# Moving attention steps of two batches to other slots of the channel MLP that hides them

## The chip, the cores and the metric

One core of a Trainium2 chip runs the whole kernel. The metric is the device time of one execution in microseconds (us). TensorE (PE) does the matrix products, VectorE (DVE), ScalarE (ACT) and GpSimd (POOL) the element-wise work, and SyncE (SP) issues nearly all DMAs.

## The reference

For 8 batches of 8 heads, 576 tokens and 64 features a head, a linear attention with cosine weights feeds an MLP-mixer block:

```python
phi(x)  = concat(relu(x) * cos_w, relu(x) * sin_w)        # 64 -> 128 features
kv, z   = sum_s phi(k) v^T,  sum_s phi(k)
attn    = (phi(q) kv) / (phi(q) z + 1e-6)                 # x: [B, 576, 512] after joining the heads
u       = x + (relu(x^T @ w_tok1) @ w_tok2)^T             # token MLP, 576 -> 256 -> 576
out     = u + relu(u @ w_ch1) @ w_ch2                     # channel MLP, 512 -> 1536 -> 512
```

## The kernel before

The 576 tokens of a batch are laid out as J = 4 full tiles of 128 rows and a half tile, so attention runs over JA = 5 tiles. The half tiles of two neighbouring batches share one tile (`u_tail`), whose channel MLP comes at the very end. All products take bf16 operands.

The channel MLP is most of the work of TensorE, and everything else is fitted between its matmuls. `channel` walks through 24 or 20 slots:

- Slots 0 to 11: one of 12 chunks of the hidden layer each. Four 128x512 matmuls fill `c_ps`, and a relu evacuates it to `h1`, on ACT for a letter "A" and on DVE for a "D" in a string given by the caller. For batch 0 that is `AAAAAAAADDAD`, for batch 1 `AAAAAADADADA`.
- The slots after: the second product into `o_ps`. In batch 0 (`wide`) all four output tiles advance together, one hidden chunk a slot (slots 12 to 23). In the other batches the tiles come one by one, six matmuls a slot, two slots a tile (12 to 19). DVE adds `u` and SP stores.

After each slot, `step()` calls the hooks registered for it. The hooks are the attention and token-MLP steps of the batches to come. In this document "channel p" is the channel MLP of batch p; in its hooks `n` is batch p+1, whose attention and token MLP have to be complete when channel p ends, and `m` (called `n2` in channel 0) is batch p+2, which is prepared. The schedule is manual, so each engine runs its instructions in the order in which they are written, and a waiting instruction holds up all that is written after it for its engine.

The steps of a batch, as methods of `Batch`:

- `k_feature(j)`: two DVE instructions that build the cosine and sine halves of `kp` for tile j. `q_feature(j)`: the same for `qp`, both halves on ACT, or one of them on DVE with `dve=(1,)`.
- `v_cast(j, eng)`: casts one tile of v to bf16, on POOL unless another engine is named.
- `q_turn(j, n)`: transposes `qp` into `qpT`. Batches 2 to 7 do it by DMA from SP; batch 1 does it on TensorE into a PSUM tile of pool `psA`, which ACT then copies (L256).
- `kv_mm`: 40 small matmuls into `kv_ps` (pool `psA`) and one evacuation by ACT (L270). It needs all five tiles of `kp` and of the cast v.
- `num(j)`: 8 matmuls into `nm` (pool `psA`), then three DVE instructions that divide and write `x`.
- `mix1(j)`, `mix1_out`: the first product of the token MLP, accumulated over the tiles, and its relu `B1`.
- `mix2(g)`: the second product into `u_ps`; DVE adds x, POOL casts to `ub`, and `ub` is transposed into `uT`, the operand of the next channel's first product. Batches 2 to 7 transpose it by DMA (L371), batch 1 on TensorE with a copy by ACT (`u_turn`, L375 and L376).

The pool `psA` has two buffers of two banks, `psM` four of one bank. `qp`, `kp` and `ub` have one buffer each, `qpT`, `x`, `u` and `uT` two. The raw v is one tile for all batches; raw k and q have two.

Of the kernel before, what the change touches and what calls it, by code (L numbers as in the profile page):

```python
# [9 lines left out]
F32 = mybir.dt.float32  # L10
# [5 lines left out]
def kernel(  # L16
# [11 lines left out]
    nc = tc.nc  # L28

    B, H, S, D = q.shape  # L30
    Dm = H * D
    _, D_tok = moe_w_tok1.shape
    _, D_ch = moe_w_ch1.shape
    P = 128
    J = S // P
    JA = J + 1
# [4 lines left out]
    NCH = D_ch // P  # L41
# [3 lines left out]
    U_PE = (1,)  # L45
# [4 lines left out]
    def first(c):  # L50

        return (0, JA - c)

    def count(c, par):
        return JA if par == c else J
# [6 lines left out]
    psM = ctx.enter_context(tc.tile_pool(name="psM", bufs=4, space=bass.MemoryType.PSUM))  # L62
# [87 lines left out]
    for par_ in range(2):  # L150
        n, f = count(0, par_), first(0)[par_]
        d = nc.gpsimd.dma_start(out=w1[0][par_::2, :n],
                                in_=moe_w_tok1.rearrange("(m r) t -> m r t", r=R)[:, f:f + n, :])
# [6 lines left out]
    for g in range(3):  # L160
        cs = slice(g * D_ch // 3, (g + 1) * D_ch // 3)
        wc1_dma.append(nc.gpsimd.dma_start(out=wc1[:, :, cs],
                                           in_=moe_w_ch1[:, cs].rearrange("(n p) c -> p n c", p=P)))
    wc2 = const.tile([P, NCH, Dm], BF16, name="wc2")
# [5 lines left out]
    for c in range(2):  # L170
        for par_ in range(2):
            n, f = count(c, par_), first(c)[par_]
# [203 lines left out]
            nc.scalar.copy(dst, tr)  # L376


    def channel(uT, u, store, by_slot, hooks, wide=False):
        h1 = one.tile([P, NCH, 4 * P], BF16, name="h1")  # L380
        slot = 0

        def step():
            nonlocal slot
            for f in hooks.get(slot, ()):
                f()
            slot += 1

        for mi in range(NCH):
            c_ps = psM.tile([P, 4, P], F32, name="c_ps", tag="psM")  # L390
            for ki in range(NCC):
                nc.tensor.matmul(c_ps, wc1[:, ki, mi * P:(mi + 1) * P], uT[:, :, ki, :],  # L392
                                 start=(ki == 0), stop=(ki == NCC - 1))
            src = c_ps.rearrange("p a b -> p (a b)")
            if by_slot[mi] == "A":
                nc.scalar.activation(h1[:, mi, :], src, AF.Relu)  # L396
            else:
                nc.vector.tensor_relu(h1[:, mi, :], src)
            step()
        if wide:  # L400
            o_ps = [psM.tile([P, Dm], F32, name="o_ps", tag="psM") for j in range(4)]
            for ki in range(NCH):
                for j in range(4):
                    nc.tensor.matmul(o_ps[j], h1[:, ki, j * P:(j + 1) * P], wc2[:, ki, :],  # L404
                                     start=(ki == 0), stop=(ki == NCH - 1))
                step()
            for j in range(4):
                nc.vector.tensor_add(u[:, j, :], o_ps[j], u[:, j, :])
                store(j, u)
            return  # L410
        for j in range(4):
            o_ps = psM.tile([P, Dm], F32, name="o_ps", tag="psM")
            for half in range(2):
                for ki in range(half * NCH // 2, (half + 1) * NCH // 2):
                    nc.tensor.matmul(o_ps, h1[:, ki, j * P:(j + 1) * P], wc2[:, ki, :],  # L415
                                     start=(ki == 0), stop=(ki == NCH - 1))
                if half:
                    nc.vector.tensor_add(u[:, j, :], o_ps, u[:, j, :])  # L418
                    store(j, u)
                step()  # L420

    def out_rows(b, par, j, n):
        f = first(b % 2)[par] + j
        return out[b].rearrange("(m r) c -> m r c", r=R)[:, f:f + n, :]

    def store_batch(b):
        def store(j, u):
            if j % 2:
                for par in range(2):
                    nc.sync.dma_start(out=out_rows(b, par, j - 1, 2), in_=u[par::2, j - 1:j + 1, :])  # L430
        return store

    def store_tail(j, u):
        for c, eng in ((0, nc.sync), (1, nc.scalar)):
            eng.dma_start(out=out_rows(2 * j + c, c, J, 1), in_=u[c::2, j:j + 1, :])


    bt = [Batch(b) for b in range(B)]
# [33 lines left out]
    def first_hooks(n, n2):  # L472
        h = {}

        def at(slot, f, *a, **kw):
            h.setdefault(slot, []).append(lambda: f(*a, **kw))
        for g in range(3):
            at(1 + g, bt[0].mix2, g, turn=False)
        for j in range(JA):
            at(3 + j, n.k_feature, j)  # L480
            at(7 + j, n.q_feature, j, dve=(1,))
            at(9, n.v_cast, j)
        at(10, n.q_turn, 0, 2)
        at(11, n.q_turn, 2, 2)
        at(11, load, 2, "v")
        at(12, n.q_turn, 4, 1)
        at(12, n.kv_mm)
        for j in range(JA):
            at(13 + j, n.num, j)
            at(15 + j, n.mix1, j)  # L490
        at(19, n.mix1_out, split=True)
        for g in range(3):
            at(20 + g, n.mix2, g)
        at(20, n2.q_feature, 0)
        at(21, n2.q_feature, 1)
        at(21, load, 3, "k")
        at(21, load, 3, "q")
        return h

    def second_hooks(n, m):  # L500
        h = {}

        def at(slot, f, *a, **kw):
            h.setdefault(slot, []).append(lambda: f(*a, **kw))
        for j in range(JA):
            at(j, n.k_feature, j)
            at(j, n.v_cast, j)
        for j in range(2, JA):
            at(j - 2, n.q_feature, j)
        at(0, n.q_turn, 0, 2)  # L510
        at(1, n.q_turn, 2, 2)
        at(2, n.q_turn, 4, 1)
        at(5, n.kv_mm)
        at(5, load, 3, "v")
        at(5, load, 4, "k")
        at(5, load, 4, "q")
        for j in range(JA):
            at(6 + j, n.num, j)
            at(8 + j, n.mix1, j)
            at(6 + j, m.q_feature, j)  # L520
            at(7 + j, m.v_cast, j)
            at(13 + j, m.k_feature, j)
        at(12, m.q_turn, 0, 2)
        at(12, n.mix1_out)
        at(13, m.q_turn, 2, 2)
        at(13, load, 4, "v")
        for g in range(3):
            at(13 + g, n.mix2, g)
        at(16, m.q_turn, 4, 1)
        return h  # L530

    def hooks_for(n, m, nxt):

        h = {}

        def at(slot, f, *a, **kw):
            h.setdefault(slot, []).append(lambda: f(*a, **kw))
        if nxt is not None:
            at(0, load, nxt, "k")
            at(0, load, nxt, "q")  # L540
            at(9, load, nxt, "v")
        if n is not None:
            at(0, n.kv_mm)
            for j in range(JA):
                at(2 + j, n.num, j)
            for j in range(JA):
                at(7 + j // 3, n.mix1, j)
            at(8, n.mix1_out)
            at(10, n.mix2, 0)
            at(11, n.mix2, 1)  # L550
            at(12, n.mix2, 2)
        if m is not None:
            for j in range(JA):
                at(3 + j, m.v_cast, j)
                at(9 + j, m.q_feature, j)
                at(13 + j, m.k_feature, j)
            at(12, m.q_turn, 0, 2)
            at(15, m.q_turn, 2, 2)
            at(16, m.q_turn, 4, 1)
        return h  # L560

    evac = ["A"] * 7 + ["D", "A", "D", "D", "D"]
    for p in range(B):
        s = bt[p]
        if p == 0:
            channel(s.uT, s.u, store_batch(p), list("AAAAAAAADDAD"), first_hooks(bt[1], bt[2]), wide=True)
            if 1 in U_PE:
                bt[1].u_turn(0)
                bt[1].u_turn(1)
        elif p == 1:  # L570
            channel(s.uT, s.u, store_batch(p), list("AAAAAADADADA"), second_hooks(bt[2], bt[3]))
        else:
            n = bt[p + 1] if p + 1 < B else None
            m = bt[p + 2] if p + 2 < B else None
            nxt = p + 3 if p + 3 < B else None
            channel(s.uT, s.u, store_batch(p), evac if n else ["A", "D"] * 6, hooks_for(n, m, nxt))
    channel(uT_tail, u_tail, store_tail, ["A", "D"] * 6, {})

    _ = tile, bass_utils
# [30 lines left out]
```

## Time and profile before

| | |
|---|---|
| median of 3 runs | 285.31 us (284.68 to 285.60) |
| span of the profiled execution | 282.6 us |
| busy: PE, DVE, ACT, POOL | 264.9, 167.2, 118.8, 56.4 us |
| channel 0, from its first matmul to that of channel 1 | 25.79 to 63.51 us |
| channel 1 | 63.51 to 98.41 us |
| channel 2 | 98.41 to 126.17 us |
| channel 3 | 126.17 to 153.75 us |

Times in the trace are us from the start of the span. A line of the timeline gives the start, the length, the engine, the line of the kernel, the operation and how many instructions were merged; in brackets stands how long the engine had been idle, and which engine's instruction released it. A line of waits gives who waited for whom, the total, the number of waits and the longest. A line of windows gives, for a stretch, its length, the busy time of each engine with its number of instructions, the clock granted to TensorE as a share of full speed, and the DMA load.

### The profile page before, as it was taken

To read this page: it belongs to the slowest core of one execution; us is meant where nothing else is said; L and a number is where in the kernel's file an instruction comes from. 1 tells how busy PE (TensorE), PEld (TensorE's weight loads), DVE (VectorE), ACT (ScalarE), POOL (GpSimd) and SP (SyncE) were. 2 spreads that over 40 slices of the span, in tenths; PEclk is the share of its full clock that TensorE was granted. 3 is DMA by queue.
4 is the path that set the end of the run, shared out by engine and by line. 5 is a ranking of instruction groups with operands and counts; after the bars stand their busy time and mean duration, and the time that the engine had idled before them with its cause. 6 is when DMAs were issued, how large, how long until landed. Compare 5 with 4: busy or idle time off the path is not lost.

```text
span 282.6 us, 4609 instructions
## 1 busy us (share of the span) xinstructions
PE 264.9 (94%) x1801; PEld 131.6 (47%) x1822; DVE 167.2 (59%) x331; ACT 118.8 (42%) x175; POOL 56.4 (20%) x83
## 2 busy tenths in 40 slices
PE   8979998979789899999999999999999999999993
PEld 2554455445333364446445544554455444444441
DVE  4774883587638645985587659665747553423321
ACT  2873493258590055805570556156515201301300
POOL 4472360052042400530061006100200120000000
PEclk9999999999997999999999999999999999999999
DMA  6999997998999999399969994940691063003012
GB/s 212 321 156 269 362 220 212 359 303 227 196 367 224 299 281 340 76 194 247 364 145 213 294 317 96 206 128 2 110 249 53 0 95 149 1 26 125 0 74 75
DMA packets 78567, 53.62 MB, mean 190 GB/s; under 512 B 47761, under 2 KB 75729, under 8 KB 78545
## 3 DMA queue, kind: packets, MB, share of 16 engines
q1 hardware_dynamic: 74608, 49.06, 62.8%
q0 software_dynamic: 3616, 3.74, 8.4%
q10 hardware_dynamic: 320, 0.52, 0.5%
q8 instruction: 14, 0.23, 0.3%
q14 instruction: 9, 0.07, 0.1%
HBM read 35.78 MB, written 9.44 MB: 160 GB/s over the span
## 4 chain that ended last, share of the span: by engine, by line
PE 65%; DMA 2%; ACT 1%; DVE 1%; POOL 0%; SPq 0%; issue 0%; DVEq 0%
PE o_ps L415 26%; PE c_ps L392 26%; PE u_ps L343 4%; PE nm L280 2%; PE kv_ps L265 2%; DMA uT<-ub 2%; PE ut_ps L355 1%; PE b_2301 L300 1%; PE b_1986 L300 1%; PE b_2606 L300 1%; PE b_1671 L300 1%; PE b_1352 L300 1%; DVE u L345 0%; POOL ub L348 0%; SPq L371 0%
## 5 line engine op out<-in xcount | busy, mean ns | idle before, releaser
L392 PE MATMUL c_ps<-uT,wc_135 128*128 128x512 bf16 x384 | 93.4, 379 | 2.9 <-ACT uT L376 1.6
L392 PEld LDWEIGHTS <-wc_135 128*128 128x128 bf16 x432 | 39.7, 98 | 45.8 <-DMA uT<-ub 1.8
L348 POOL CAST ub<-u 128x1024 bf16<-128x1024 f32 x14 | 14.7, 1049 | 129.0 <-DVE u L345 74.0
L418 DVE TENSOR_TENSOR u<-o_ps,u 128x512 f32<-128x512 f32 x28 | 19.3, 689 | 23.9 <-PE o_ps L415 23.8
L288 DVE TENSOR_TENSOR x<-nm,den 128x512 bf16<-128x512 f32 x40 | 27.7, 692 | 1.4
L345 DVE TENSOR_TENSOR u<-u_ps,x 128x1024 f32<-128x1024 f32 x16 | 19.5, 1222 | 6.0 <-PE u_ps L343 6.0
L284 DVE TENSOR_SCALAR den<-nm 128x8 f32<-128x8 f32 x40 | 6.6, 166 | 27.0 <-PE nm L280 27.0
L280 PEld LDWEIGHTS <-qpT 128*128 128x128 bf16 x320 | 14.8, 98 | 13.5 <-issue 2.8
L280 PE MATMUL nm<-kv,qpT 128*128 128x65 bf16 x320 | 16.8, 194 | 2.9 <-ACT kv L270 1.4
L236 ACT ACTIVATE qp<-qt_79,bias_108,cos_t 128x512 bf16<-128x512 f32 x20 | 15.9, 804 | 3.5 <-DMA qpT<-qp 3.5
L223 POOL CAST vbf_125<-vt_77 128x512 bf16<-128x512 f32 x20 | 13.6, 723 | 16.7 <-DMA vt_77<-in_v_dram 15.3
L236 ACT ACTIVATE qp<-qt_76,bias_108,cos_t 128x512 bf16<-128x512 f32 x19 | 15.0, 803 | 0.5 <-DMA qt_76<-in_q_dram 0.5
L415 PE MATMUL o_ps<-wc_139,h_844 128*128 128x512 bf16 x47 | 12.2, 401 | 1.4 <-ACT h_844 L396 1.3
L396 ACT ACTIVATE h_1186<-c_ps 128x512 bf16<-128x512 f32 x8 | 4.8, 597 | 19.6 <-issue 14.3
L265 PEld LDWEIGHTS <-kp 128*128 128x128 bf16 x320 | 11.1, 97 | 3.3 <-ACT qpT L256 1.2
L138 PE MATMUL wm<-zero 128*128 128x512 bf16 x37 | 11.0, 467 | 1.4 <-POOL zero L70 1.3
L396 ACT ACTIVATE h_2730<-c_ps 128x512 bf16<-128x512 f32 x6 | 3.6, 597 | 20.6 <-PE c_ps L392 20.6
L236 ACT ACTIVATE qp<-qt_76,bias_108,sin_t 128x512 bf16<-128x512 f32 x15 | 12.0, 803 | 0.0
L236 ACT ACTIVATE qp<-qt_79,bias_108,sin_t 128x512 bf16<-128x512 f32 x15 | 12.0, 801 | 0.0
L404 PE MATMUL o_ps<-wc_139,h_441 128*128 128x512 bf16 x45 | 11.8, 379 | 0.2
L215 DVE TENSOR_SCALAR kp<-kt_75,cos_t 128x512 bf16<-128x512 f32 x18 | 10.3, 571 | 2.5 <-DMA kt_75<-in_k_dram 2.5
L215 DVE TENSOR_SCALAR kp<-kt_78,sin_t 128x512 bf16<-128x512 f32 x20 | 11.0, 551 | 0.0
(146 smaller groups left out, 394.0 us busy)
## 6 DMA issues: line engine op xcount, KB each, us to landing
out_dram<-u SPq DMA_DIRECT2D x32, 256.0 KB, 2.6
vt_77<-in_v_dram SPq DMA_DIRECT2D x8, 640.0 KB, 9.2
vt_77<-in_v_dram SPq DMA_DIRECT2D x8, 512.0 KB, 9.0
kt_75<-in_k_dram SPq DMA_DIRECT2D x4, 640.0 KB, 6.8
qt_76<-in_q_dram SPq DMA_DIRECT2D x4, 640.0 KB, 9.4
kt_78<-in_k_dram SPq DMA_DIRECT2D x4, 640.0 KB, 7.2
qt_79<-in_q_dram SPq DMA_DIRECT2D x4, 640.0 KB, 9.3
kt_75<-in_k_dram SPq DMA_DIRECT2D x4, 512.0 KB, 5.2
```

What stands on the lines that cost most here:

```text
L215: eng.tensor_scalar(dst, src, scalar1=tab, scalar2=0.0, op0=ALU.mult, op1=ALU.max)
L223: eng.tensor_copy(self.vb[:, j, :, :D], src)
L236: nc.scalar.activation(self.qp[:, j, :, f, :], src, AF.Relu, bias=bias0, scale=tab[:, self.c, j:j + 1])
L265: nc.tensor.matmul(kv_ps[:, g, hh * (D + 1):(hh + 1) * (D + 1)], self.kp[:, j, h].rearrange("p f d -> p (f d)"), self.vb[:, j, h, :D + 1], ...
L280: nc.tensor.matmul(nm[:, h // HH, c0:c0 + D + 1], lw, self.kv[:, h, :D + 1], start=True, stop=True)
L288: nc.vector.tensor_mul(self.x[:, j, :].rearrange("p (g h d) -> p g h d", g=2, h=HH), nmv[:, :, :, :D], den_b)
L300: nc.tensor.matmul(self.b1[mi], w1[self.c][:, j, mi * P:(mi + 1) * P], self.x[:, j, :], start=(j == 0), stop=(j == J))
L345: nc.vector.tensor_add(self.u[:, js, :], u_ps, self.x[:, js, :])
L348: nc.gpsimd.tensor_copy(self.ub[:, js, :], self.u[:, js, :])
L392: nc.tensor.matmul(c_ps, wc1[:, ki, mi * P:(mi + 1) * P], uT[:, :, ki, :], start=(ki == 0), stop=(ki == NCC - 1))
L415: nc.tensor.matmul(o_ps, h1[:, ki, j * P:(j + 1) * P], wc2[:, ki, :], start=(ki == 0), stop=(ki == NCH - 1))
L418: nc.vector.tensor_add(u[:, j, :], o_ps, u[:, j, :])
```

## The change

The change moves hooks of channel 0 and channel 1 to other slots. No operation is added or taken away in the work that runs. Its aim is to put work that isn't urgent (features and turns of a later batch) behind what TensorE waits for, and to spread the casts of v.

In channel 0: q features of batch 1 one slot earlier; its v casts in slot 10 in place of 9, with tiles 0 to 2 on POOL, tile 3 on DVE and tile 4 on ACT; `kv_mm` ahead of the second and third q turn, in slot 11 in place of 12; `num`, `mix1`, `mix1_out` and `mix2` one slot earlier; the two `u_turn` of batch 1 inside the last two slots, where they had come after the whole channel.

In channel 1: the q features of batch 3 in slots 13 to 17, behind the last relu evacuation of slot 11, where they had stood in slots 6 to 10 between the evacuations; its q turns in slots 15, 17 and 18 (12, 13 and 16 before); its k features one slot later.

It also gives `channel` an argument `fine` and `store_tail` an argument `cs`. No call sets `fine`, and `cs` keeps its default, so neither changes an instruction. They are left out below.

```diff
@@ first_hooks (channel 0; n is batch 1, n2 is batch 2)
         for j in range(JA):
             at(3 + j, n.k_feature, j)
-            at(7 + j, n.q_feature, j, dve=(1,))
-            at(9, n.v_cast, j)
-        at(10, n.q_turn, 0, 2)
+            at(6 + j, n.q_feature, j, dve=(1,))
+            at(10, n.v_cast, j, (nc.gpsimd, nc.gpsimd, nc.gpsimd, nc.vector, nc.scalar)[j])
+        at(9, n.q_turn, 0, 2)
+        at(11, n.kv_mm)
         at(11, n.q_turn, 2, 2)
-        at(11, load, 2, "v")
+        at(12, load, 2, "v")
         at(12, n.q_turn, 4, 1)
-        at(12, n.kv_mm)
         for j in range(JA):
-            at(13 + j, n.num, j)
-            at(15 + j, n.mix1, j)
-        at(19, n.mix1_out, split=True)
+            at(12 + j, n.num, j)
+            at(14 + j, n.mix1, j)
+        at(18, n.mix1_out, split=True)
         for g in range(3):
-            at(20 + g, n.mix2, g)
-        at(20, n2.q_feature, 0)
-        at(21, n2.q_feature, 1)
+            at(19 + g, n.mix2, g)
+        at(19, n2.q_feature, 0)
+        at(20, n2.q_feature, 1)
         at(21, load, 3, "k")
         at(21, load, 3, "q")
+        if 1 in U_PE:
+            at(22, n.u_turn, 0)
+            at(23, n.u_turn, 1)
@@ second_hooks (channel 1; n is batch 2, m is batch 3)
             at(8 + j, n.mix1, j)
-            at(6 + j, m.q_feature, j)
             at(7 + j, m.v_cast, j)
-            at(13 + j, m.k_feature, j)
-        at(12, m.q_turn, 0, 2)
+            at(14 + j, m.k_feature, j)
         at(12, n.mix1_out)
-        at(13, m.q_turn, 2, 2)
         at(13, load, 4, "v")
         for g in range(3):
             at(13 + g, n.mix2, g)
-        at(16, m.q_turn, 4, 1)
+        for j in range(JA):
+            at(13 + j, m.q_feature, j)
+        at(15, m.q_turn, 0, 2)
+        at(17, m.q_turn, 2, 2)
+        at(18, m.q_turn, 4, 1)
@@ the loop over the channels
-            if 1 in U_PE:
-                bt[1].u_turn(0)
-                bt[1].u_turn(1)
```

More of the change, by code (lines that the diff above doesn't have):

```diff
@@ L376, in u_turn, with channel @@
             nc.scalar.copy(dst, tr)
-    def channel(uT, u, store, by_slot, hooks, wide=False):
+    def channel(uT, u, store, by_slot, hooks, wide=False, fine=False):
         h1 = one.tile([P, NCH, 4 * P], BF16, name="h1")
@@ L411, in channel @@
         for j in range(4):
+            if fine and j == 3:
+                for cs in (slice(0, Dm // 2), slice(Dm // 2, Dm)):
+                    o_ps = psM.tile([P, Dm // 2], F32, name="o_ps", tag="psM")
+                    for ki in range(NCH):
+                        nc.tensor.matmul(o_ps, h1[:, ki, j * P:(j + 1) * P], wc2[:, ki, cs],
+                                         start=(ki == 0), stop=(ki == NCH - 1))
+                    nc.vector.tensor_add(u[:, j, cs], o_ps, u[:, j, cs])
+                    store(j, u, cs)
+                break
             o_ps = psM.tile([P, Dm], F32, name="o_ps", tag="psM")
@@ L431, in store_batch, with store_tail @@
         return store
-    def store_tail(j, u):
+    def store_tail(j, u, cs=slice(0, Dm)):
         for c, eng in ((0, nc.sync), (1, nc.scalar)):
-            eng.dma_start(out=out_rows(2 * j + c, c, J, 1), in_=u[c::2, j:j + 1, :])
+            eng.dma_start(out=out_rows(2 * j + c, c, J, 1)[:, :, cs], in_=u[c::2, j:j + 1, cs])
     bt = [Batch(b) for b in range(B)]
```

## The prediction, made before the changed kernel ran

> **What bounds the kernel now.** I first read the page's busy times (PE 94% of the span), then its 40 slices, to see where PE is not busy.
>
> ```profile
> PE   8979998979789899999999999999999999999993
> ACT  2873493258590055805570556156515201301300
> PEclk9999999999997999999999999999999999999999
> DMA  6999997998999999399969994940691063003012
> ```
>
> Each slice is 7.07 us. From slice 14 on (99 us) PE is full; before it there are holes, and slice 12 (85 to 92 us) has a lower clock. The windows by channel give their size. The four lines are channels 0, 1, 2 and 3:
>
> ```profile
> 25.79:63.51 37.72, 34.05 (x258) 17.79 (x262) 24.72 (x46) 19.69 (x26) 10.46 (x14) 1.00 1.02 296
> 63.51:98.41 34.90, 30.02 (x193) 13.88 (x196) 23.34 (x47) 17.23 (x27) 8.70 (x15) 0.95 1.02 261
> 98.41:126.17 27.76, 27.65 (x195) 14.02 (x198) 18.74 (x36) 13.44 (x20) 7.46 (x11) 1.00 0.83 228
> 126.17:153.75 27.58, 27.48 (x196) 13.90 (x196) 18.47 (x36) 13.44 (x20) 5.52 (x7) 1.00 0.91 241
> ...
> 85.33:88.74 3.41, 3.41 (x9) 1.18 (x9) 2.58 (x5) 0.00 (x0) 0.17 (x1) 0.50 1.23 222
> ```
>
> Channel 1 does the matmul work of channel 3 in 34.90 us instead of 27.58. So 7.3 us are to be had there at most; anything won before 98 us carries to the end, since PE is full afterwards. The last line shows one piece of it: 3.41 us at half clock, 1.7 us lost.
>
> PE's waits in channel 1, then PE and ACT in the timeline around 80 us, name the rest:
>
> ```profile
> PE c_ps L392 <- ACT uT L376: 1.6, 1, 1.6
> PE nm L280 <- ACT kv L270: 1.4, 1, 1.4
> PE c_ps L392 <- DMA uT<-ub: 1.3, 1, 1.3
> PE o_ps L415 <- ACT h_844 L396: 1.3, 1, 1.3
> PE u_ps L343 <- ACT B_1093 L309: 0.5, 1, 0.5
> ```
>
> ```profile
> 81.85 1.24 PE L415 MATMUL o_ps<-wc_139,h_844 128*128 128x512 bf16 x5
> 84.41 0.39 PE L415 MATMUL o_ps<-wc_139,h_844 128*128 128x512 bf16 x1 [1.32 <-ACT h_844 L396]
> 85.32 1.86 PE L343 MATMUL u_ps<-B_1093,w_140 128*128 128x512 bf16 x4 [0.52 <-ACT B_1093 L309]
> ...
> 75.75 0.81 ACT L236 ACTIVATE qp<-qt_79,bias_108,cos_t 128x512 bf16<-128x512 f32 x1 [3.46 <-DMA qpT<-qp]
> ...
> 83.07 0.80 ACT L236 ACTIVATE qp<-qt_79,bias_108,sin_t 128x512 bf16<-128x512 f32 x1
> 83.78 0.58 ACT L396 ACTIVATE h_844<-c_ps 128x512 bf16<-128x512 f32 x1
> 84.25 1.01 ACT L309 ACTIVATE B_1093<-b_1007 128x1024 bf16<-128x1024 f32 x1
> ```
>
> ACT sat 3.46 us at batch 3's first q feature, until batch 2's DMA turns released the single `qp`. Ten features, 0.70 us apart, then ran in front of the relus of chunks 7, 9 and 11 and of B1. The last relu's input was complete at 79.7 us, its relu ran at 83.78. PE stands still for 1.32 and 0.52 us, and the half clock follows.
>
> [...] the window before it, 81.92 to 85.33, was still 46% busy (PE 1.58 of 3.41 us)[...] here a DVE feature of 0.47 us takes about 0.78 while POOL casts.
>
> **Channel 1, part by part.**
>
> *q features to slots 13 to 17.* The relus of chunks 7, 9, 11 now find ACT empty; chunk 11's ends at about 80.35, long before PE wants it. mix1 ends near 81.8, so B1 (1.01 us) is ready at 82.9. PE runs six o_ps matmuls from 81.85 (6 x 0.216 = 1.30), to 83.15, and starts `u_ps` there instead of at 85.32: 2.17 us saved. [...] the 1.70 us of lost clock go too. Sum 3.87. The features themselves (10 x 0.70 = 7.0 us, 82.9 to 90) lie on an ACT that was idle from 85.3 to 99.5. DVE's relus are untouched.
>
> *q turns behind the uT turns on SP.* SP is in order, and the queue of transfers is busy here (DMA share over 1). Before, two q turns stood ahead of the v load and of both uT turns: the v load was issued at 89.92, uT at 91.44, and uT landed at 98.4, so PE waited 1.33. Now the v load waits only for POOL's casts of v3, which end at 83.6, and the uT turns follow it. `u_ps` of g = 1 now ends at 86.3 (83.15 + 2 x 0.865 + 1.30, and 0.1 of drain). Then: DVE, with batch 3's first k features ahead of it and slowed by POOL's cast, adds until 88.3; POOL casts to 89.4; SP issues to 90.6; landing 3.2 us after issue (the median of the 12 uT turns) gives 92.7 to 93.8. From the side of the queue: 98.4 less the two q turns that went ahead (89.6 and 92.0 were their landings, some 4.2 us together) is 94.2. PE is ready at 86.2 + 1.30 + 0.43 + 24 x 0.216 = 93.1. I take 93.9 for channel 2's first matmul: 4.5 us earlier than 98.41, 0.8 of the wait left; ends 93.1 and 95.0.
>
> *Late q turns.* SP issues them at about 91.9, 94.0 and 96.1; a landing takes 4.5 us (median of the q turns), so 96.4, 98.5 and 100. Channel 2's `num` 0, 2 and 4 come 3.9, 6.1 and 8.4 us after its start: 97.8, 100.0 and 102.3. Hidden, with 1.4 us or more of slack. If a turn takes 6 us, `num` stalls by 0.1; at the 10.4 us maximum, by 4.5. I take 0.
>
> *k features one slot later.* DVE has about 7.3 us of work between 87.1 and the end of the channel, and `kv_mm` of channel 2 wants them at 94.8. Hidden, barely: 0.
>
> *What stays.* The 1.36 us wait for `kv` at 71 us: ACT's chain of relus and batch 2's features from 64.57 to 71.68 isn't edited.
>
> **Channel 0.** *kv ahead of the turns, v on three engines.* Before, kv started at 43.72 after 1.06 us for a `psA` buffer (the ACT copy of the second turn), and a turn had waited 0.36 for DVE. After, on before's clock: chunk 9 ends at 37.0; turn 0 to 37.9, without a wait (its q features are done at 36.95); chunks 10 and 11 to 39.5. kv can start. But v lands at 37.5, so POOL's three casts of 0.8 end at 40.05. DVE reaches v3 after q3's half, at 40.2 (0.4 to 0.7 us long, the range of the first batch's DVE casts): 40.7. ACT reaches v4 after three more steps: copy of turn 0, 38.3 to 40.1; relu 10 to 40.6; q4 to 41.3; v4, 0.62 by the first batch's ACT casts, to 41.9. So kv's last fifth waits for ACT, until 41.95, and ends at 42.2. Behind it in PE's queue stand turn 1 (to 43.35), o_ps chunk 0 (44.2), the last turn (44.7) and `num` 0. That one needs a `psA` buffer, which turn 1's copy (1.86 us from 43.5) gives back at 45.4. Then `num` 2 ends at 48.5 with three o_ps chunks done; before, it ended at 48.9 with four. One chunk is 0.865, so channel 0 is 0.45 us *behind* there: its stalls moved, they didn't go. From `num` 2 to `mix2` both orders have the same pitch (1.65 us a slot, one free `psA` buffer).
>
> *u turns into the last slots.* Before, both copies (1.02 us each) followed the last matmul; now the first lies beside the last o_ps chunk. PE: two turns and 1.57 idle before (60.89 to 63.51, 2.62 us); after, 0.45 of turn moved ahead, and 0.66 + 1.02 + 0.05 behind: 0.44 saved. Sum of channel 0: +0.45 - 0.44 = 0, between -1.1 (kv finds v ready) and +1.5 (ACT or DVE a step later).
>
> **Sum.** 285.31 - 3.87 - 0.63 (the part of the uT wait and its order that goes) + 0 = 280.8 us.
>
> **The rivals.**
> 1. *The transfers take over* (0.20). DMA share is above 1 all through channel 1; uT lands at 95.0 and channel 0 loses 0.8. Gain 3.4 - 0.8 = 2.6: 282.7 us. Against it: two turns leave the queue ahead of uT.
> 2. *Everything fits* (0.12). uT at 93.1 and channel 0 ahead by 0.5 to 1: gain 5.3 + 0.7 = 6.0: 279.3 us.
> 3. *Not faster* (0.06). kv's wait for ACT and the wait of `num` 0 [...] halve the clock (1.7), channel 0 loses 1.5 on top, and the late turns stall `num` in channel 2 by 1.5: 4.7 against 4.5 gained: 285.5 us or more. For it: slack of only 1.4 us. Against it: all three must happen[...].
>
> **How the numbers follow.** The forecast has 0.62. The range 279.3 to 283.1 takes in rival 2, rival 1 and their spread. Faster is the forecast, rivals 1 and 2: 0.93 with roundings; 0.02 for the same and 0.05 for slower from rival 3.
>
> **What would show it.** Right: no q feature of batch 3 before B1 on ACT, no PE wait for the relu or B1 in channel 1, clock 1.00 throughout, channel 1 about 30.4 us long with the 1.36 wait for `kv` still in it; in channel 0 a wait of kv for the ACT cast near 41 us and of `num` 0 for the copy near 45, and channel 1's start within 1 us of 63.5. Wrong: a half-clock window anywhere between 40 and 100 us, uT landing 2 us after PE is ready, or `num` of channel 2 waiting for `qpT`.

## The result: slower, by a wait that the forecast did not have

The changed kernel takes 287.93 us (286.99 to 288.07, 4 runs) against 285.05 us before (284.68 to 285.60, 4 runs): ratio 1.0092, 95% interval 1.0063 to 1.0121. The loss is small, 0.9%, but clear of the noise. The forecast was 280.8 us, with 283.1 as its upper end.

Its profiled execution spans 285.2 us. The slices of the page, as before 7 us each:

```profile
PE   8979989989089999999999999999999999999993
PEclk9999999999779999999999999999999999999998
DMA  6999998709999998999989994960693063003012
```

There is one hole in PE, slice 10 (71 to 78 us), with a lower clock there and in slice 11 (7 tenths in both). In DMA there is a hole too, and it comes first: slice 8, from 57 to 64 us, has a load of 0. In the kernel before, slice 8 had a 9 there.

The windows of channels 0 and 1 of the changed kernel (length; PE, PEld, DVE, ACT, POOL busy; clock; DMA share; GB/s):

```profile
25.79:63.40 37.61, 34.46 (x264) 17.96 (x263) 25.50 (x48) 20.51 (x28) 9.63 (x13) 1.00 0.82 232
63.40:101.30 37.90, 29.41 (x196) 14.18 (x196) 21.73 (x43) 17.58 (x27) 9.13 (x14) 0.91 1.05 279
```

Channel 0 is about as long as before. The window begins at 25.79 us, where the channel began before; here its first matmul is at 26.02, so that it took 37.38 us in place of 37.72. Channel 1 grew from 34.90 to 37.90. What PE waits for from channel 0 to channel 2:

```profile
PE nm L280 <- DMA qpT<-qp: 8.5, 1, 8.5
PE c_ps L392 <- ACT uT L376: 1.1, 1, 1.1
PE kv_ps L265 <- ACT vbf_125 L221: 0.6, 1, 0.6
PE nm L280 <- ACT qpT L256: 0.6, 1, 0.6
PE kv_ps L265 <- DVE vbf_125 L223: 0.4, 1, 0.4
PE u_ps L343 <- DVE B_758 L307: 0.3, 1, 0.3
```

All four waits of channel 1 that the forecast went after (relu, B1, uT, and the half clock behind them) are absent. In their place `num` 0 of channel 1 waits 8.5 us for batch 2's q turn. No edit touches that turn: it is still in slot 0 of channel 1. SP's timeline shows what happened to it; first the changed kernel, then the kernel before:

```profile
61.99 1.28 SPq L365 DMA_TRANSPOSE uT_tail<-utb  x1
63.32 1.29 SPq L87 DMA_DIRECT2D kt_78<-in_k_dram  x2
64.66 1.33 SPq L87 DMA_DIRECT2D qt_79<-in_q_dram  x2
66.09 3.20 SPq L439 DMA_DIRECT2D out_dram<-u  x4
69.39 11.70 SPq L242 DMA_TRANSPOSE qpT<-qp  x3
```

```profile
49.88 3.58 SPq L87 DMA_DIRECT2D kt_78<-in_k_dram  x2
53.56 3.10 SPq L87 DMA_DIRECT2D qt_79<-in_q_dram  x2
62.50 1.28 SPq L365 DMA_TRANSPOSE uT_tail<-utb  x1
```

The loads of batch 3's k and q were in slot 21 in both kernels. But `mix2(2)` of batch 1 ends with a DMA of its own, the transpose of `utb` (L365), and the change moved that from slot 22 to slot 21, where it is registered ahead of the loads. In this trace SP issued in the order of the program: the transpose waited until 61.99 us for POOL's cast of `utb` (61.35 to 61.96), and the loads stood behind it. So 2.36 MB of loads (two of 640 KB and two of 512 KB) were issued at 63.3 in place of 49.9. The windows from 56 to 63 us show the transfers standing still in the changed kernel (first) and running in the kernel before (second):

```profile
56.00:63.00 7.00, 6.29 (x41) 3.28 (x40) 5.71 (x7) 3.94 (x6) 3.73 (x5) 1.00 0.02 6
```

```profile
56.00:63.00 7.00, 5.56 (x37) 3.03 (x37) 5.50 (x8) 3.86 (x6) 3.22 (x5) 1.00 1.00 331
```

DMA share 0.02 against 1.00, 6 GB/s against 331.

### The profile page after: what moved, and what is told of

It reads as the page before. It is cut to its first block, busy times and chain, and to the rows that moved or that the text cites. A ratio compares the mean times of both kernels' runs of the same rounds, so it can differ in the third digit from the quotient of the medians.

```text
span 285.2 us, 4624 instructions
## 1 busy us (share of the span) xinstructions
PE 265.5 (93%) x1822; PEld 131.9 (46%) x1822; DVE 168.4 (59%) x332; ACT 119.8 (42%) x176; POOL 55.8 (20%) x81
## 4 chain that ended last, share of the span: by engine, by line
PE 81%; DMA 7%; ACT 7%; DVE 3%; issue 1%; POOL 0%; ACTq 0%; POOLq 0%; DVEq 0%
PE c_ps L392 30%; PE o_ps L424 29%; PE u_ps L343 5%; PE nm L280 4%; DMA qpT<-qp 3%; DMA vt_77<-in_v_dram 3%; PE o_ps L404 3%; ACT qp L236 2%; PE kv_ps L265 2%; ACT qpT L256 2%; DVE x L288 1%; PE ut_ps L355 1%; PE b_692 L300 1%; PE b_1001 L300 1%; PE b_2301 L300 1%; PE b_1986 L300 1%
## 5 line engine op out<-in xcount | busy, mean ns | idle before, releaser
L223 POOL CAST vbf_125<-vt_77 128x512 bf16<-128x512 f32 x18 | 12.2, 719 | 25.3 <-DMA vt_77<-in_v_dram 23.8
L215 DVE TENSOR_SCALAR kp<-kt_78,sin_t 128x512 bf16<-128x512 f32 x20 | 12.5, 625 | 0.0
L404 PE MATMUL o_ps<-wc_139,h_441 128*128 128x512 bf16 x48 | 12.3, 379 | 0.0
L215 DVE TENSOR_SCALAR kp<-kt_75,cos_t 128x512 bf16<-128x512 f32 x18 | 10.3, 570 | 2.8 <-DMA kt_75<-in_k_dram 2.8
L215 DVE TENSOR_SCALAR kp<-kt_78,cos_t 128x512 bf16<-128x512 f32 x20 | 11.3, 563 | 0.0
```

Source lines behind the costliest of these rows:

```text
L215: eng.tensor_scalar(dst, src, scalar1=tab, scalar2=0.0, op0=ALU.mult, op1=ALU.max)
```

## The experiments

**1. Undo the inversion, keep all the rest; and make the inversion alone.** Four kernels side by side, the kernel before on the same chip at 286.07 us (284.63 to 288.46, 23 runs). The first edit, `e1_loads_first`:

```diff
+        at(21, load, 3, "k")
+        at(21, load, 3, "q")
         for g in range(3):
             at(19 + g, n.mix2, g)
...
-        at(21, load, 3, "k")
-        at(21, load, 3, "q")
```

> The changed kernel, with the loads of batch 3's k and q written ahead of mix2 of batch 1, so that SP issues them before the tail's transpose, as the kernel before did. Theory A (the whole loss is that these two loads came to stand behind the tail's transpose on SP, were issued 13 us later, and lay in the transfer queue ahead of batch 2's q turns): the q turns land before 73 us again, num 0 of channel 1 waits only the 1.4 us for kv, no half-clock window, and the rest of the change gives what was forecast: 279.5 to 281.8 us. Rival B (the moved steps themselves crowd the transfers in channel 1): num still waits several us for qpT, time above 284.

Measured: 279.58 us (278.92 to 280.21), ratio 0.9788 (0.9756 to 0.9821), as theory A has it. PE's waits in channels 1 and 2:

```profile
PE nm L280 <- DMA qpT<-qp: 1.6, 2, 1.4
PE c_ps L392 <- ACT uT L376: 1.1, 1, 1.1
PE c_ps L392 <- DMA uT<-ub: 0.5, 1, 0.5
```

and the windows 56 to 63 us and channel 1:

```profile
56.00:63.00 7.00, 6.45 (x41) 3.38 (x41) 5.50 (x8) 3.56 (x6) 3.41 (x5) 1.00 1.06 350
63.72:94.03 30.31, 28.34 (x197) 13.51 (x196) 22.42 (x45) 17.58 (x27) 8.28 (x13) 1.00 1.01 265
```

The transfers are busy again, the clock is 1.00, and channel 1 takes 30.31 us. The expectation was wrong in one thing: the 1.4 us of `num` 0 are now put down to the turn, not to kv. ACT's copy of kv ends at 72.50 and `num` 0 starts at 72.59, so the two end within 0.1 us of each other.

The reverse, `e2_before_loads_late`, is the kernel before with only this:

```diff
-        at(21, load, 3, "k")
-        at(21, load, 3, "q")
+        at(22, load, 3, "k")
+        at(22, load, 3, "q")
```

> The kernel before, with nothing changed but the slot of the loads of batch 3's k and q: 22 in place of 21, which puts them behind the tail's transpose on SP. Theory A: num 0 of channel 1 waits some 8 us for qpT and two windows run at half clock; batch 3's q features on ACT also wait for the same turns and then hold up relus as before: 293 to 297 us. Rival B (the order of the loads costs nothing by itself): 284.5 to 286.

Measured: 293.65 us (292.85 to 295.37), ratio 1.0289 (1.0244 to 1.0334), again theory A. The order of two loads by itself costs 7.6 us:

```profile
PE nm L280 <- DMA qpT<-qp: 7.9, 1, 7.9
PE c_ps L392 <- DMA uT<-ub: 3.7, 1, 3.7
```

The uT wait of the kernel before grows here from 1.3 to 3.7 us. The relus, by contrast, cost PE only 0.2 us in this run, though they still stood behind the q features; why was not tried.

**2. The two halves of the change.** `e3_channel0_alone` has the hooks of channel 0 as changed (loads first) and those of channel 1 as before; `e4_channel1_alone` has channel 0 wholly as before and the changed channel 1:

```diff
-            at(6 + j, m.q_feature, j)
             at(7 + j, m.v_cast, j)
-            at(13 + j, m.k_feature, j)
-        at(12, m.q_turn, 0, 2)
+            at(14 + j, m.k_feature, j)
...
+        for j in range(JA):
+            at(13 + j, m.q_feature, j)
+        at(15, m.q_turn, 0, 2)
...
```

> Only the part of the change in channel 0, with the loads ahead of the tail's transpose; channel 1 as before. Theory A (channel 0's moves shift its stalls and give nothing): 284.3 to 285.8 us, channel 1 starting at the same time within 0.3 us. Rival C (kv ahead of the turns is worth the 1.06 us wait that it removes, and the u turns 0.4): 283.5 us.

> Only the part of the change in channel 1; channel 0 and all its loads as before. Theory A (the q features behind the relus and the q turns behind the uT turns carry all of the gain): 280 to 281.5 us, no wait for a relu or B1 and no half-clock window in channel 1, a wait for uT of at most 1.3 us. Rival D (the late q turns of batch 3 make num of channel 2 wait, or uT still lands late): 282.5 or more, with the wait named in the trace.

Measured: channel 0 alone 286.39 us (20 runs), ratio 1.0002 (0.9974 to 1.0030): no change. The time lies above the 284.3 to 285.8 us expected, as the kernel before did when measured beside it (286.07). Channel 1 alone 280.44 us, ratio 0.9816 (0.9778 to 0.9854): the gain, and about as much as both together (0.9788); their intervals overlap. In channel 1 of the second kernel no wait for a relu or B1 is left, the clock is 1.00, and the wait for uT is 0.3 us:

```profile
64.10:94.08 29.98, 28.33 (x197) 13.58 (x196) 22.55 (x45) 17.58 (x27) 8.68 (x14) 1.00 1.01 268
```

Channel 1 of the first kernel, with channel 0 alone changed, shows something that the forecast did not separate:

```profile
63.77:99.16 35.39, 28.66 (x197) 13.46 (x196) 22.81 (x46) 17.23 (x27) 8.29 (x14) 1.00 1.04 258
```

No half clock falls in this channel (1.00 in the line above, 0.993 over the whole run), and yet it takes 35.39 us, where the kernel before takes 34.90 with 3.41 us at half clock in it. PE waits 3.9 us for uT here, in place of 1.3. So in this trace the half clock that went gave nothing as long as uT landed late. The q features and the q turns of batch 3 were moved together in every run but the one of experiment 4, so how the gain divides between them is not shown.

**3. Ahead in the queue, or just late?** Up to here the 8.5 us could come from loads lying *ahead* of the q turns in the queue. `e5_loads_after_turns` takes them out of the way:

```diff
-        at(21, load, 3, "k")
-        at(21, load, 3, "q")
...
         at(2, n.q_turn, 4, 1)
+        at(2, load, 3, "k")
+        at(2, load, 3, "q")
```

> The changed kernel, with the loads of batch 3's k and q not earlier but later still: in slot 2 of channel 1, behind batch 2's three q turns on SP. Theory A (what costs is that 2.4 MB lay in the transfer queue ahead of the turns, not that the loads were late): the turns land by 75 us or earlier and num waits 1.4 us or up to 3; k and q of batch 3 are wanted only from slot 13 on and come in time; 279 to 282.5 us. Rival E (late loads cost by themselves, since v of batch 3 and k and q of batch 4 queue up behind them and uT behind those): num doesn't wait, but a later wait takes its place, on uT or v, and the time is above 284.

Measured: 287.98 us (287.38 to 288.31), ratio 1.0057 (1.0027 to 1.0086), as slow as the changed kernel. This is rival E, and theory A as it stood falls. The turns were in time (`num` 0 waits only the 1.4 us for kv), and the wait came back in another place, this time on uT:

```profile
PE c_ps L392 <- DMA uT<-ub: 7.5, 1, 7.5
PE nm L280 <- ACT kv L270: 1.4, 1, 1.4
```

POOL's timeline shows how the late loads reach uT:

```profile
89.17 3.42 POOL L223 CAST vbf<-vt 128x512 bf16<-128x512 f32 x5 [24.23 <-DMA vt<-in_v_dram]
92.53 2.40 POOL L348 CAST ub<-u 128x1024 bf16<-128x1024 f32 x2
```

The v of batch 3 came in behind the late loads. POOL waited for it until 89.17 us (81.21 with the loads first), and batch 2's `ub` casts stand behind the casts of v in POOL's program, though DVE had added `u` by 87.47. So the uT turns were issued from 93.79 on, in place of 87.02.

I put the theory anew (A2): the transfers have little time to spare from 45 to about 100 us (share 1.02 over channel 0 and over channel 1 before, although only 0.69 and 0.84 in the two windows from 60 to 70 us), and a stretch in which they stand still comes back as a wait of PE of about the same length, at the place where a late transfer holds up an engine. Here the stretch is again 56 to 63 us, with a share of 0.01. Two such places were seen, the q turns and POOL's `ub` casts. That the wait would come back whatever the order is not shown: a kernel with the `ub` casts ahead of the v casts was not run. A2 says that half the loads in time should give half the wait. `e9_k_first_q_late` leaves only q's load behind the transpose:

```diff
+        at(21, load, 3, "k")
         for g in range(3):
             at(19 + g, n.mix2, g)
...
-        at(21, load, 3, "k")
         at(21, load, 3, "q")
```

> The changed kernel with the load of batch 3's k ahead of the tail's transpose, and that of its q left behind it. Theory A2 (the queue of transfers has no time to spare up to channel 2, and every us that it stands idle between 53 and 63 us comes back as a wait of TensorE): half of the 2.4 MB fills about half of the idle stretch, so num 0 waits 4 to 5.5 us for qpT in place of 8.5, and the time lies about midway between the changed kernel and that with both loads first, 282.5 to 285 us. Rival H (one load behind the transpose is as bad as two): 287 or more; or one is hidden by slack: below 281.

Measured: 283.42 us (283.19 to 283.88), ratio 0.9889 (0.9815 to 0.9963), as A2 has it. The share from 56 to 63 us was 0.41, and the wait:

```profile
PE nm L280 <- DMA qpT<-qp: 4.0, 1, 4.0
```

Share 0.02, 0.41 and 1.06 in that window give waits of 8.5, 4.0 and 1.4 us at `num` 0, of which kv alone would take the last 1.4.

**4. The order of the turns in channel 1.** The forecast had part of its gain from q turns that follow the uT turns. `e11_turn_before_uT` puts one of them back in front of the second:

```diff
-        for g in range(3):
-            at(13 + g, n.mix2, g)
         for j in range(JA):
             at(13 + j, m.q_feature, j)
-        at(15, m.q_turn, 0, 2)
+        at(14, m.q_turn, 0, 2)
+        for g in range(3):
+            at(13 + g, n.mix2, g)
```

> Loads first, with batch 3's first q turn in slot 14 of channel 1, ahead of the second uT turn on SP, in place of slot 15 behind it. If the order of the turns in the queue matters as the prediction said, uT lands about 2 us later and channel 2's first matmul waits 2 to 3 us for it in place of 0.5: 281 to 282.5 us. Rival I (the uT turn is held by POOL's cast in any case, and the q turn fits in ahead): no more than 280.2.

Measured: 281.61 us (280.84 to 283.12), ratio 0.983 (0.9761 to 0.9898), and a uT wait of 2.1 us in place of 0.5:

```profile
PE c_ps L392 <- DMA uT<-ub: 2.1, 1, 2.1
```

SP issued the second uT turn at 92.24 us, behind the q turn (88.61, 3.54 us long), though its `ub` was cast by 89.3. So the order counts in this trace. The time agrees with the expectation, but the interval reaches that of the kernel with the loads first, the execution traced was the slowest of the four (283.12 us), and the share from 56 to 63 us was 0.85 in it. How much of the time is due to the order stays open.

**5. Making it better.** `e7_casts_on_pool` undoes the spreading of the v casts, on top of the loads first:

```diff
-            at(10, n.v_cast, j, (nc.gpsimd, nc.gpsimd, nc.gpsimd, nc.vector, nc.scalar)[j])
+            at(10, n.v_cast, j)
```

> The kernel with the loads first, with all five v casts of batch 1 on POOL in slot 10, in place of three there, one on DVE and one on ACT. By the working of the prediction kv waited for the ACT cast, which stands behind a 1.86 us copy, until 41.95; POOL casts five in 3.4 us (the kernel before), from 37.6 to 41.1, so kv ends 0.8 us earlier and channel 1 starts 0.5 to 0.8 earlier: 278.8 to 279.4 us. Rival F (spreading the casts is what lets kv go ahead of the turns): kv waits longer, 280.5 or more.

Measured: 278.53 us (278.17 to 279.73), ratio 0.9744 (0.9711 to 0.9777) to the kernel before in the same session (286.08 us). This is a little below the 278.8 to 279.4 us expected. In its trace kv no longer waits for a cast. By time it can't be told from the loads first alone (0.9756 to 0.9821).

The traces of the ten kernels with the changed channel 0 tell more, once they are sorted by when POOL begins to cast the v of batch 1, which differs between executions. Where it began at 36.6 to 37.4 us, channel 0 took 36.01 us from its first matmul with all casts on POOL (two kernels) and 37.37 to 37.38 with the casts spread (five kernels): 1.4 us for keeping them on POOL. Where POOL began only at 39.3 to 39.7 us, it took 37.75 us with all on POOL (one kernel) and 37.66 and 37.67 spread (two kernels), so the placing made no difference.

`e6_early_turn_kv_dve` issues batch 2's first turn before the tail's transpose and evacuates kv on DVE in channel 1. `e10_pool_casts_kv_dve` has the casts on POOL and kv on DVE, `e8_both` all three edits:

```diff
+        at(21, n2.q_turn, 0, 2)        # e6, e8
...
-        at(0, n.q_turn, 0, 2)          # e6, e8
-        at(5, n.kv_mm)
+        at(5, n.kv_mm, nc.vector.tensor_copy)
```

> The kernel with the loads first, with batch 2's first q turn issued in slot 21 of channel 0, ahead of the tail's transpose and the stores (it stood behind them, in slot 0 of channel 1), and the evacuation of kv in channel 1 on DVE, which is idle there, in place of ACT, where it stands behind six relus. The 1.4 us that num 0 waits go: 277.9 to 278.6 us. Rival G (only one of the two was the wait, and the turns of tiles 2 and 3, still behind the stores, make num 2 wait in its place): 279 or more.

> Loads first, all five v casts on POOL, and the evacuation of kv in channel 1 on DVE; batch 2's first turn stays behind the stores. The 1.4 us wait of num 0 for kv goes if the turn lands by then: 277.2 to 278.2 us against 278.5 for the casts alone. By A2, channel 2 can't start before its uT has come through the queue, so a wait for uT of up to 1 us may take part of it back: then 277.8 to 278.6.

> The two edits before together, on top of the kernel with the loads first. If they are independent, their gains add: 277.0 to 278.2 us; if channel 0's gain is eaten by a wait for the loads of batch 2 or for a turn, about the better one of the two alone.

Measured: 278.76 us (0.9738, 0.9699 to 0.9777), 278.82 us (0.9741, 0.9671 to 0.9810) and 279.13 us (0.9758, 0.9730 to 0.9787). All three lie above the ranges expected. None differs from the casts on POOL by more than the intervals, and the gains do not add. In the trace of `e6_early_turn_kv_dve` `num` 0 of channel 1 no longer waits for kv or for the turn. In that of `e10_pool_casts_kv_dve` the kv wait went and a wait for the turn of the same length took its place:

```profile
PE nm L280 <- DMA qpT<-qp: 1.7, 2, 1.5
PE c_ps L392 <- ACT uT L376: 1.1, 1, 1.1
```

In the kernel with all three, `num` in channel 1 waits only 0.2 us, yet the total is no lower: v came late in the execution traced (POOL began to cast at 39.26 us), kv of channel 0 waited 0.7 us for POOL, and uT was waited for 0.5 us. The early turn, issued at 58.35 us, can't be the cause of the kv wait. The lowest median is that of the changed kernel with the loads first and the casts on POOL, 2.6% faster than before; it can't be told from the other three by time.

## Why the prediction was wrong

**The step that failed** is the sum of 0 for channel 0, because of a term that it left at nothing. In the part on channel 0 the forecast followed PE, ACT, DVE and POOL through the moved slots, and summed the channel to 0; it never walked SP's list there. `mix2` was costed as matmuls, a DVE add and a POOL cast and the uT turns; that its last part issues one more DMA, for the tail, was in no step and had no price. Moving it one slot set it ahead of two loads in the same slot. The sum lacked a term for that, and the term measured 7.6 us on the kernel before (286.07 to 293.65) and 8.4 us on the changed kernel (279.58 to 287.93, in different sessions).

In the trace of the changed kernel: 8.5 us of wait and 1.4 us of half clock (2.76 us of work, 79.34 to 82.10, at 0.50) came in; 1.36 for kv, 0.23 for x, 1.32 and 0.52 for relu and B1, 1.33 for uT and 1.71 of half clock went out. That is 9.9 less 6.5, or 3.4 us, and channel 1 grew by 3.0.

**Rival 1 had the right resource and the wrong place.** It said that the transfers take over, at 282.7 us, through uT. They did, at the turns of batch 2. What stood against it ("two turns leave the queue ahead of uT") was true and did not help: seven idle us far ahead of uT decided. The DMA row of the page and the share over 1 were read as a risk for uT alone, though they gave reason to look for *any* idle stretch of the transfers before 100 us. Rival 3, the one that ended slower, was wrong in all three of its terms. That two waits in channel 0 would halve the clock was an estimate; the clock granted in channel 0 was 1.00.

**The rest of channel 0, right.** The forecast was 0 us from the moved kv, casts and u turns. Channel 0 alone gave a ratio of 1.0002, which by itself says little, since uT landed late there. The lengths of the channel say more: 37.66 us there and 37.38 in the changed kernel, against 37.72 before. The waits came where they were put: in the changed kernel kv waited 0.40 us for the DVE cast and 0.65 for the ACT cast, ending near 42.3 (forecast 42.2), `num` 0 waited 0.64 for the copy and began at 45.35 (45.4), the wait behind the u turns fell from 1.57 to 1.10. The spread casts, which the change brought in as a help, cost the 1.4 us of experiment 5 where v came early.

**Channel 1, right in its length.** With the loads in their place, channel 1 takes 30.31 us (forecast 30.4), the half clock is gone (granted clock 1.00), PE waits 0.5 us for uT (forecast 0.8), and batch 3's late turns cost 0.15 us in channel 2 (forecast 0). The slack of 1.4 us that the forecast gave these turns was not there: SP issued the first at 93.37 us, not at 91.9, and in no kernel with the changed channel 1 and the loads in time did they cost more than 0.22 us. The parts of the sum, 3.87 us for the features and the clock and 0.63 for uT, were not measured apart. That the half clock goes with the waits was an estimate from the one stretch of 3.41 us at 0.50; on what the granted clock depends was not shown. In the traces channel 1 gave 34.90 - 30.31 = 4.6 us, where 4.5 were forecast. By the ratio, 0.9788 of 286.07, it was 6.1 (5.1 to 7.0). The executions of the kernel before in that session lay between 284.63 and 288.46, with a mean clock of 0.986 to 0.997; those of the kernel with the loads first kept 0.998 or more. One stretch of 3.41 us at 0.50 in a span of 282.6 us makes a mean of 0.994, as in the execution traced. So, as an estimate from these means, a gain beyond 4.6 fits time at half clock that differs between the executions of the kernel before. That can't be all of it: at one and the same mean clock, 0.994, that kernel took 285.39 to 287.39 us. What else differs was not tried.

## What to carry to other kernels

When a step is moved, list every instruction that it issues, DMAs included, and walk each queue that issues in order (here SP's, where the loads came at 63.3 us in place of 49.9), past the moved step and the ones that share its slot: a transfer that waits for data must not come to stand ahead of loads that wait for nothing. Here that order, alone, cost 7.6 us on the kernel before. Where the transfers are full over a long stretch (here a share of 1.02 over channels 0 and 1 before), treat their idle time as part of the critical path: look for the last us in which nothing is in flight, not for the transfer that is waited for. Here, moving that one out of the way only moved the wait, of 8.5 us for the q turn, to one of 7.5 us for uT, behind POOL, which a late load held up.

## What the runs showed of the hardware that I had not expected

In the changed kernel 3.41 us with no matmul in them (71.86 to 75.27) were followed by 6.83 us at half clock (75.27 to 82.10), with matmuls in them from 79.34 on:

```profile
71.86:75.27 3.41, 0.00 (x0) 0.00 (x0) 0.00 (x0) 0.31 (x1) 0.00 (x0) 1.00 1.41 375
75.27:78.68 3.41, 0.00 (x0) 0.00 (x0) 0.00 (x0) 0.00 (x0) 0.00 (x0) 0.50 0.91 140
78.68:82.10 3.42, 2.76 (x21) 1.61 (x22) 1.06 (x3) 0.39 (x1) 0.00 (x0) 0.50 1.12 214
```

So most of the 6.8 us at half clock fell on an idle PE and cost nothing. The price was the 1.4 us named above, an estimate: half of the 2.76 us that PE was busy. The length of a stretch at half clock is therefore not its cost here; the work that falls into it is.
